# The last down projection in seven-product form with 128 by 256 accumulators, and the activation moved to where the up products leave PSUM

## The chip, the cores and the metric

The kernel runs on one core of a Trainium2 chip. The metric is device time in microseconds (us), the median of several executions; lower is better. The engines are TensorE (PE, with its weight loads as PEld), VectorE (DVE), ScalarE (ACT), GpSimd (POOL) and SyncE (SP, which issues most DMAs).

## The reference

Attention with a memory term gives 2304 tokens of 512 values; two feed-forward blocks follow. All arithmetic is float32.

```python
# x: [2304, 512] from attention
g = x @ moe_w_gate                                   # 512 -> 1536
x = (g * sigmoid(g) * (x @ moe_w_val)) @ moe_w_out   # 1536 -> 512
h = x @ moe2_w_in                                    # 512 -> 2048
h = where(h >= 1, h, where(h <= -1, 0, (h + 1)**2 / 4))
out = h @ moe2_w_out                                 # 2048 -> 512: the stage that is changed
```

## The kernel before, in words

Every float32 operand of a product is split into a high part (a cast to fp32r) and a low part (the rest), and each product is three fp32r matmuls (`PARTS`: low by high, high by low, high by high). The cast is made on ACT, the subtraction of the rest on DVE; `halves` and `split` do that.

After attention and a little early work the kernel has three long stages.

1. Gate and value products, from about 284 us: each block of 256 by 256 by (2 times 384 tokens) is made with seven products in place of eight (Strassen's scheme in Winograd's form): `chain` issues products 1 to 7 on PE, ACT copies partial sums from one PSUM bank to another, DVE adds. A chain takes three of the eight PSUM banks. `pair` prepares the weights (unpacks the numbers, makes four sums, splits).
2. Down products of the first block (`down`, line L1621), then `y_pieces`, which makes the seven sums of each token block.
3. The second block: up products by `chain` with kind "up" (L1540), 8 pairs `p` of weight columns by 3 token blocks `kb`; in its function `last` two of the four outputs are copied from PSUM by ACT (L1589), the others are already in SBUF, and `store` writes 48 tiles to DRAM (`h2s`). Then the last down projection, `down2`, for 6 groups of 384 tokens and 8 pairs `i` of hidden rows: load a tile back (L1659), Relu and Square on ACT (L1661, L1663), the clamping minimum on DVE (L1664), split (L1440 on ACT, L1443 on DVE), and 18 matmuls of 128 by 512 (L1675) into three banks. At the end of a group three copies (L1690) and stores. Its 16 weight blocks were unpacked, split and put in DRAM earlier (`parked`), and are read back whole (`whole`).

The order of all instructions is written out beforehand. A class `Plan` simulates the engines with fixed costs (for PE `e_pe(n, cols)`: n times (cols + 32)/2.4 ns, with 25 in place of 32 below 320 columns) and handover times (`LAT`), keeps the matmuls in the order of the program (`seq`), and gives every other instruction a due time worked back from the matmul that needs it, or from `by`. `gate(ahead)` holds a load back until PE is that many ns before its use. Each engine then runs its list in order, so a waiting instruction holds up those behind it. SBUF places are counted by tags: 25 places `X` of 6 KB for split operands, 7 flat tiles `T`, `raw`, `rw`, `wp`, `wA` for preparing weights, `su` for the chains' sums, and eight banks `mm`.

Of the kernel before, what the change touches and what calls it, by code (L numbers as in the profile page):

```python
# [19 lines left out]
P = 128  # L20
# [23 lines left out]
SET_AHEAD, PARK_AHEAD, H_AHEAD, H2_AHEAD, W_AHEAD, W2_AHEAD = 40000, 60000, 20000, 20000, 12000, 7000  # L44
# [107 lines left out]
class Plan:  # L152
# [4 lines left out]
    LAT = {"PE": 220, "ACT": 165, "DVE": 150, "POOL": 120, "SP": 650, "DMA": 950}  # L157
# [783 lines left out]
class Weights:  # L941
# [174 lines left out]
    def whole(self, plan, u, gate):  # L1116
        i = plan.inst("X")
        s = {"i": [i]}

        def load():  # L1120
            s["w"] = self.slab(i.slot, [P, 2, 512])
            self.nc.sync.dma_start(f32(s["w"]), u["home"])

        s["t"] = [plan.dma(None, [1456], load, [u["store"]], [i], behind=gate)]
        return s

    def pair(self, plan, srcs, behind, free, homes=None):
# [4 lines left out]
        places = [plan.inst("X"), plan.inst("X"), plan.inst("wh")]  # L1132
        s, w = {}, {}
        n = 2 * 512

        def load(j):
            if j == 0:
                s["raw"] = self.p["rw"].tile([P, 2 * n], U32, name="rw", tag=f"rw{i_raw.slot}")
            dst = s["raw"][:, j * n:(j + 1) * n].rearrange("p (k c) -> p k c", k=srcs[j].shape[1])
            nc.sync.dma_start(dst, srcs[j])  # L1140
# [47 lines left out]
        sub, add = nc.vector.tensor_sub, nc.vector.tensor_add  # L1188
# [4 lines left out]
                ("DVE", e_dve2(n), sign, [i_raw, i_W]), ("DVE", e_dve2(n), whole, [i_W]),  # L1193
                ("DVE", e_dve2(256), two(add, 4, 2, 3), [i_W]), ("DVE", e_dve2(256), two(sub, 2, 0, 2), [i_W]),
                ("DVE", e_dve2(256), two(sub, 5, 4, 0), [i_W]), ("DVE", e_dve2(256), two(sub, 6, 1, 5), [i_W]))
        for k, (on, took, fn, uses) in enumerate(steps):
            if homes and k < 6:
                continue
            t = [plan.add(on, took, None, fn, t, uses)]
            made[k] = t[0]  # L1200
        ends = [self.split(plan, None, [made[d]], lambda a=a, b=b: f32(W(a, b)), lambda j=j, m=(b - a) * 256: dst(j)[:, :, 0:m],
                           (b - a) * 256, [i_W, places[j]], behind=free)
                for j, (d, a, b) in enumerate(((7, 0, 3), (8, 3, 6), (9, 6, 7)))]
        at_ = ((0, 0), (0, 256), (2, 0), (1, 0), (1, 256), (1, 512), (0, 512))
        return {"t": [ends[j] for j, _ in at_], "i": [places[j] for j, _ in at_],
                "k": lambda k, part, j: w[at_[k][0]][:, part, at_[k][1] + j * P:at_[k][1] + (j + 1) * P]}

# [24 lines left out]
def tile_attention_two_moe(  # L1232
# [12 lines left out]
    nc.gpsimd.memset(half, 0.5)  # L1245
    xs = dram.tile([P, KT, NT], F32, name="xs")
    gv = [dram.tile([P, 2, GE * HB], F32, name=f"gv{j}") for j in range(2)]
    hs = [[dram.tile([P, 2, HB], F32, name=f"hs{i}_{g}") for g in range(NG)] for i in range(F1 // 2)]
    h2s = [[dram.tile([P, 2, HB], F32, name=f"h2s{i}_{g}") for g in range(NG)] for i in range(F2 // 2)]
# [118 lines left out]
    mm = ctx.enter_context(tc.tile_pool(name="mm2", bufs=1, space=PSUM, reuse_waits="tile"))  # L1368
    unused = [early[g][0]["slot"] for g in range(1, GE, 2)]
# [156 lines left out]

    def chain(S, x, kind, ends):
# [21 lines left out]
        def spot(name, place, j):  # L1549

            def get():
                if kind == "up":
                    return rt["get"]()[:, j]
                if name not in s:
                    s[name] = su.tile([P, HB], F32, name=name, tag=f"su{place.slot}")
# [17 lines left out]
        def last():  # L1573
# [4 lines left out]
            done = {0: [], 1: []}  # L1578
            for n, (T, j, src, i, t) in enumerate(parts):
# [232 lines left out]
```

## Time and profile before

| what | value |
|---|---|
| median of 3 runs | 1013.84 us (1013.26 to 1015.34) |
| the profiled execution's own time | 1013.86 us |
| its span in the profile | 1012.1 us |
| granted TensorE clock, mean | 0.996 of full speed |
| up products of the second block | 637.5 to 811.2 us |
| last down stage | 811.2 to 1008.2 us |

The profiled execution is 1.76 us longer than its span. Line numbers in the profile are those of the kernel before.

### The profile page before, as it was taken

Reading aid. Unit: us, or ns where it says so; the run is one execution under the profiler, and the core shown is the slowest. Engines: PE = TensorE matmul, PEld = TensorE weight load, DVE = VectorE, ACT = ScalarE, POOL = GpSimd, SP = SyncE. Lnnn points to the kernel's source line nnn. Section 1 sums busy time; section 2 is a strip of 40 time slices with the busy share of each in tenths; the row PEclk is TensorE's granted clock in tenths of the full one; section 3 lists DMA queues with packets and bytes.
Section 4 is the critical chain, followed back from the end, with each engine's and each line's share of the span. In section 5 each row is a group of like instructions: output and inputs, shape, how many; then the busy total and the mean of one; then the engine's idle time right before and its main releaser. Section 6 shows DMA issues by size and latency. Waiting matters only on the chain.

```text
span 1012.1 us, 16215 instructions
## 1 busy us (share of the span) xinstructions
PE 995.0 (98%) x5898; PEld 907.0 (90%) x5898; DVE 678.4 (67%) x1402; ACT 621.4 (61%) x1221; POOL 116.8 (12%) x165
## 2 busy tenths in 40 slices
PE   6999999999999999999999999999999999999998
PEld 6667787778999999999999999999999988888886
DVE  5899998872888878676467577776654346455541
ACT  3999888873566665655255445666554657566651
POOL 3543666630000000000000000000000000000000
PEclk9999999999999999999999999999999999999999
DMA  7867454214835463544975544356742696324430
GB/s 182 192 160 181 129 128 115 75 60 132 291 103 183 146 197 134 169 169 159 397 273 186 183 146 162 141 201 230 256 179 116 214 384 205 125 80 139 141 95 31
DMA packets 137248, 171.72 MB, mean 170 GB/s; under 512 B 67536, under 2 KB 99280, under 8 KB 137168
## 3 DMA queue, kind: packets, MB, share of 16 engines
q1 hardware_dynamic: 135838, 170.39, 51.5%
q8 instruction: 46, 0.75, 0.3%
q10 hardware_dynamic: 1330, 0.30, 0.2%
q14 instruction: 34, 0.28, 0.1%
HBM read 111.28 MB, written 59.38 MB: 169 GB/s over the span
## 4 chain that ended last, share of the span: by engine, by line
PE 92%; DMA 3%; ACT 2%; DVE 1%; SPq 1%; issue 0%; ACTq 0%; DVEq 0%
PE mm L1540 38%; PE mm L1675 19%; PE mm L1621 15%; PE av L911 4%; PE s L730 3%; PE mm L1317 3%; PE t L861 2%; PE av L903 2%; PE s L764 2%; DMA xr<-xs 1%; PE t L878 1%; ACT a L751 1%; DMA qn<-in_q_dram 1%; PE t L839 1%; PE tk L609 1%; PE tq L620 1%
## 5 line engine op out<-in xcount | busy, mean ns | idle before, releaser
L1540 PE MATMUL mm<-xw 128*128 128x384 f32 x1944 | 346.9, 334 | 1.4 <-ACT mm L1562 1.0
L1540 PEld LDWEIGHTS mm<-xw 128*128 128x128 f32 x1944 | 337.7, 188 | 2.2 <-ACT mm L1562 1.3
L1675 PE MATMUL mm<-xw 128*128 128x512 f32 x864 | 196.2, 389 | 0.0
L1675 PEld LDWEIGHTS mm<-xw 128*128 128x128 f32 x864 | 162.2, 188 | 33.6
L1621 PE MATMUL mm<-xw 128*128 128x384 f32 x864 | 150.1, 334 | 0.0
L1621 PEld LDWEIGHTS mm<-xw 128*128 128x128 f32 x864 | 149.8, 188 | 0.0
L751 ACT ACTIVATE a<-a,mn 128x256 f32<-128x256 f32 (+3 forms) x128 | 71.4, 565 | 4.0 <-DVE mn L744 3.7
L1664 DVE SCALAR_TENSOR_TENSOR t<-r,t 128x768 f32<-128x768 f32 x48 | 46.0, 958 | 38.0 <-ACT t L1663 38.0
L1443 DVE TENSOR_TENSOR xw<-t,xw 128x768 fp32r<-128x768 f32 x48 | 45.9, 957 | 37.2 <-ACT xw L1440 37.2
L1440 ACT CAST xw<-t 128x768 fp32r<-128x768 f32 x48 | 40.1, 834 | 40.6 <-DVE t L1664 40.6
L1540 PE MATMUL mm<-xw,wh 128*128 128x384 f32 x324 | 64.8, 334 | 0.0
L823 POOL TENSOR_SCALAR a<-a,r,one 128x128 f32<-128x128 f32 (+4 forms) x77 | 57.9, 763 | 44.0 <-DVE r L812 22.5
L1562 ACT COPY mm<-mm 128x384 f32<-128x384 f32 x54 | 25.1, 465 | 57.1 <-PE mm L1540 56.8
L744 DVE CUSTOM_DVE_ANT_0 a<-s,mask 128x128 f32<-128x128 f32 (+3 forms) x128 | 55.6, 483 | 6.3 <-PE s L730 6.2
L1540 PEld LDWEIGHTS mm<-xw,wh 128*128 128x128 f32 x324 | 56.9, 188 | 0.0
L515 ACT COPY R<-t 128x384 f32<-128x384 f32 (+2 forms) x97 | 44.9, 507 | 8.7 <-PE t L861 5.0
L1661 ACT ACTIVATE t<-r,half 128x768 f32<-128x768 f32 x48 | 44.9, 935 | 7.9 <-DMA r<-h2s 7.2
L911 PE MATMUL av<-R,vn 128*64 128x320 f32 (+3 forms) x384 | 47.8, 379 | 0.0
L911 PEld LDWEIGHTS av<-R,vn 128*64 128x64 f32 x384 | 28.1, 137 | 20.8 <-ACT R L515 0.4
L1440 ACT CAST xw<-h 128x768 fp32r<-128x768 f32 x36 | 29.7, 835 | 27.2 <-DMA h<-hs 14.7
L1443 DVE TENSOR_TENSOR xw<-h,xw 128x768 fp32r<-128x768 f32 x36 | 34.0, 954 | 14.9 <-ACT xw L1440 14.7
L1047 DVE TENSOR_TENSOR xw<-wp,xw 128x768 fp32r<-128x768 f32 x36 | 34.0, 954 | 12.1 <-ACT xw L1045 12.0
(160 smaller groups left out, 1471.2 us busy)
## 6 DMA issues: line engine op xcount, KB each, us to landing
h2s<-r SPq DMA_DIRECT2D x48, 384.0 KB
r<-h2s SPq DMA_DIRECT2D x48, 384.0 KB
raw<-in_moe_w_out_dram SPq DMA_DIRECT2D x28, 512.0 KB
park<-pk SPq DMA_DIRECT2D x28, 512.0 KB
hs<-h SPq DMA_DIRECT2D x33, 384.0 KB
h<-hs SPq DMA_DIRECT2D x33, 384.0 KB
xw<-park SPq DMA_DIRECT2D x24, 512.0 KB
xr<-xs SPq DMA_DIRECT2D x24, 384.0 KB
```

What stands on the lines that cost most here:

```text
L515: copy(dst(), src())
L744: nc.vector.tensor_tensor_reduce(a, st[f"s{h}{tag}"][:, at_[c]:at_[c] + kl[c]], self.mask0[:, 512 - kl[c]:512], -0.125, 3.0e38, ALU.add, A ...
L751: nc.scalar.activation(a, a, AF.Exp, bias=mn[:, o:o + 1], scale=-1.0, accum_out=sm[:, o:o + 1])
L823: eng.tensor_scalar(a, a, r, self.one, op0=ALU.mult, op1=ALU.mult)
L911: nc.tensor.matmul(o[rg][halves[h], c0:c1], V, r, start=False, stop=i == len(terms[rg]) - 1, tile_position=(0, h * 64), skip_group_check=True)
L1440: nc.scalar.copy(s["x"][:, :, 0], t())
L1443: nc.vector.tensor_sub(s["x"][:, :, 1], t(), f32(s["x"][:, :, 0]))
L1540: nc.tensor.matmul(o, S["k"](k, pw, j), x[k]["at"](px, j), start=begin and not (i or j), stop=j == 1 and i == 2, skip_group_check=True)
L1621: nc.tensor.matmul(o, u["k"](pw, m), h["at"](px, j), start=(p == 0 and j == 0 and n == 0), stop=(p == F1 // 2 - 1 and j == 1 and n == 2), ...
L1661: x1 = add_act(2 * HB, lambda raw=raw, t=t: nc.scalar.activation(t["get"](), raw["get"](), AF.Relu, bias=half, scale=0.5), [x], [raw["i"], ...
L1664: x1 = add_dve(2 * HB, lambda raw=raw, t=t: nc.vector.scalar_tensor_tensor(t["get"](), raw["get"](), 1.0, t["get"](), op0=ALU.max, op1=ALU ...
L1675: nc.tensor.matmul(o, h["at"](px, j)[:, m * P:(m + 1) * P], u["w"][:, pw], start=(i == 0 and j == 0 and n == 0), stop=(i == F2 // 2 - 1 an ...
```

## The change

The last down projection becomes seven products as well. A task is now a `batch`: 256 tokens (`n`, 9 chunks) by four row blocks of 128 of the weights (`b`, 4 of them). `split` is called for 768, 768 and 256 columns; `prod` goes over 2 row blocks, the 7 products and the 3 parts. A stationary operand is a 128 by 128 piece of tokens, the moving one is a 128 by 256 piece of weights, and the seven accumulators of 128 by 256 lie in half banks, four banks to a token chunk. DVE makes four token sums for a batch (three instructions), ACT and DVE split them; the weight sums are made in advance by `parked_pair` (8 pairs, 7 pieces each), written to DRAM and read back by `seven`. `clean` fills the halves that no matmul starts with zeros, `finish` combines the seven accumulators (one copy on ACT, four additions on DVE) and stores. The first two token chunks run interleaved, the other seven one after another.

The activation goes from the reading side to the end of `chain`: `bend` makes Relu and Square on ACT and the minimum on DVE, from PSUM for two of the four outputs and in SBUF for the other two (with DVE in place of ACT for the first step where `kb` is not 0). The `h2s` tiles that are stored now hold activated values.

Other parts of it: loads of `h` in `down` and of the batches are issued by ACT in place of SP; the weight parking of the last stage goes from the stage of the gates to spots set by due times there and in the down stage of the first block; the last two pairs `p` of the up stage alternate for each `kb`; `wA` and the chains' sums share one `su` tile.

```diff
-SET_AHEAD, PARK_AHEAD, H_AHEAD, H2_AHEAD, W_AHEAD, W2_AHEAD = 40000, 60000, 20000, 20000, 12000, 7000
+SET_AHEAD, PARK_AHEAD, H_AHEAD, H2_AHEAD, W_AHEAD, W2_AHEAD = 40000, 60000, 20000, 20000, 12000, 36000
-    LAT = {"PE": 220, "ACT": 165, "DVE": 150, "POOL": 120, "SP": 650, "DMA": 950}
+    LAT = {"PE": 220, "ACT": 165, "DVE": 150, "POOL": 120, "SP": 650, "DMA": 950, "QACT": 950}
...
+    def bend(n, t, src, deps, uses, by, dst=None, act=True):
+        dst = dst or t
+        if act:
+            x = add_act(n, lambda: nc.scalar.activation(t(), src(), AF.Relu, bias=half, scale=0.5), deps, uses, by=by)
+            x = add_act(n, lambda: nc.scalar.activation(t(), t(), AF.Square), [x], uses, by=by)
+        else:
+            x = plan.add("DVE", e_dve(n), None, lambda: nc.vector.tensor_scalar(
+                t(), src(), -1.0, 1.0, op0=ALU.max, op1=ALU.add), deps, uses, by=by)
+            x = add_act(n, lambda: nc.scalar.activation(t(), t(), AF.Square, scale=0.5), [x], uses, by=by)
+        return add_dve(n, lambda: nc.vector.scalar_tensor_tensor(
+            dst(), src(), 1.0, t(), op0=ALU.max, op1=ALU.min), [x], uses, by=by)
...
+            if kind == "up":
+                for j, (src, i, t) in enumerate(((lambda: P_("e"), i_e, t2), (lambda: P_("a"), i_a, t4))):
+                    done[0].append(bend(HB, lambda j=j: lf["get"]()[:, j], src, [t], [i, lf["i"]], by))
+                tmp = flat("b2")
+                done[1].append(bend(2 * HB, tmp["get"], rt["get"], [v1, v2], [rt["i"], tmp["i"]], by, rt["get"], not ends["kb"]))
...
-    def down2(g):
...
+    BANKS = ((0, 0), (1, 0), (3, 0), (3, 256), (2, 0), (1, 256), (2, 256))
+    SEVEN = (((0, 1, 0), (1, 3, 2), (3, 2, 6)), ((6, 4, 1), (4, 5, 4), (5, 6, 5)), ((2, 7, 3),))
...
+        d = add_dve(256, lambda: sub(R(4, 5), R(0, 1), R(1, 2)), x, i_r)
+        d = add_dve(512, both, [d], i_r)
+        d = add_dve(256, lambda: sub(R(7, 8), R(3, 4), R(6, 7)), [d], i_r)
+        t = [split(j, x if j == 0 else [d]) for j in range(3)]
+        def prod(j, prods):
+            for i, u in enumerate(us):  
+                for k, g, w in prods:
+                    bk, c = BANKS[k]
+                    o = acc(state, bk)[:, c:c + 256]
+                    for q, (pw, px) in enumerate(PARTS):
+                        nc.tensor.matmul(o, dst(j)[:, px, i, g - 1 - 3 * j], u["k"](w, pw),
+                                         start=b + i + q == 0 and k in OPEN,
+                                         stop=b == 3 and i == 1 and q == 2, skip_group_check=True)
...
+        state["clean"] = [add_act(256, lambda k=k: fill(k), [], [state["i"][k]], behind=gate(8000) if w_out else seq[-1:])
+                          for k in (1, 2, 3)]
...
+        t = add_act(256, lambda: nc.scalar.copy(one_(), state[0][:, 0:256]), [ends[0]], [i_b[0], one["i"]], by=by)
+        t = add_dve(512, lambda: add(O()[:, 0:4:3], one["get"]()[:, 0:1, 0:256].to_broadcast(two), B2(1)), [t, ends[1], ends[5]],
+                    [i_b[1], one["i"], i_o], by=by)
+        t = add_dve(512, lambda: add(O()[:, 1:3], O()[:, 3:4].to_broadcast(two), B2(2)), [t, ends[4], ends[6]], [i_b[2], i_o], by=by)
+        t = add_dve(256, lambda: add(O()[:, 3], O()[:, 2], state[2][:, 0:256]), [t], [i_b[2], i_o], by=by)
+        t = add_dve(512, lambda: add(O()[:, 1:3], O()[:, 1:3], B2(3)), [t, ends[2], ends[3]], [i_b[3], i_o], by=by)
...
-    for g in range(NG):
-        down2(g)
+    for some in ((0, 1), *((n,) for n in range(2, NT // (2 * P)))):
+        for n in some:
+            clean(states[n])
+        for b in range(4):
+            for n in some:
+                ends[n] = batch(n, b, states[n], n == NT // (2 * P) - 1)
+        for n in some:
+            finish(n, states[n], ends[n], n == NT // (2 * P) - 1)
```

## Rows read from the trace of the kernel before

**Rows 1.** The page, busy time of each engine and its share of the span

```profile
PE 995.0 (98%) x5898; PEld 907.0 (90%) x5898; DVE 678.4 (67%) x1402; ACT 621.4 (61%) x1221; POOL 116.8 (12%) x165
```

**Rows 2.** Chain of waits from 486 us on: start, length, what

```profile
637.50 173.71 PE mm L1540 x1002
811.22 4.12 PE mm L1675 x18
...
816.40 191.82 PE mm L1675 x846
...
1008.24 0.69 DVE oo L1690
```

**Rows 3.** Busy time by stage, with counts; clock, DMA share and GB/s last

```profile
283.70:486.70 203.00, 203.00 (x1171) 203.00 (x1172) 154.01 (x269) 119.37 (x220) 0.00 (x0) 1.00 0.48 166
...
637.50:811.20 173.70, 173.70 (x1004) 173.65 (x1003) 101.85 (x165) 102.36 (x186) 0.00 (x0) 1.00 0.55 192
811.20:1008.20 197.00, 197.00 (x871) 162.95 (x869) 93.35 (x102) 116.61 (x142) 0.00 (x0) 1.00 0.44 149
```

**Rows 4.** Groups by shape, PE: count, busy us, mean ns of one, idle before

```profile
L1675 PE MATMUL mm<-xw 128*128 128x512 f32 x864 | 196.2, 389 | 0.0
L1621 PE MATMUL mm<-xw 128*128 128x384 f32 x864 | 150.1, 334 | 0.0
```

**Rows 5.** The same for PEld: a load for an fp32r matmul, for a transpose

```profile
L1621 PEld LDWEIGHTS mm<-xw 128*128 128x128 f32 x864 | 149.8, 188 | 0.0
...
L861 PEld LDWEIGHTS t<-ident,a 128*128 128x128 f32 x224 | 26.1, 141 | 4.3 <-PE tp L682 1.0 <-ACT a L751 0.5 <-POOL a L823 0.5
```

**Rows 6.** Chain of waits, attention, 140 to 195 us: eight transposes

```profile
186.19 0.87 PE tk L609 x8
```

**Rows 7.** Groups by shape from 637.5 us on, DVE

```profile
L1664 DVE SCALAR_TENSOR_TENSOR t<-r,t 128x768 f32<-128x768 f32 x48 | 46.0, 958 | 38.0 <-ACT t L1663 38.0
L1443 DVE TENSOR_TENSOR xw<-t,xw 128x768 fp32r<-128x768 f32 x48 | 45.9, 957 | 37.2 <-ACT xw L1440 37.2
L1569 DVE TENSOR_TENSOR r<-r,mm 128x384 f32<-128x384 f32 x24 | 13.3, 554 | 33.9 <-PE mm L1540 29.5 <-ACT pk L1045 2.0 <-ACT wA L981 1.4
...
L1175 DVE TENSOR_TENSOR wp<-wp 128x256 f32<-128x256 f32 x27 | 11.1, 421 | 0.3
L1690 DVE COPY oo<-mm 128x512 f32<-128x512 f32 x12 | 8.3, 691 | 32.5 <-PE mm L1675 32.5
...
L1160 DVE TENSOR_SCALAR wp<-wp 128x1024 f32<-128x1024 f32 x6 | 4.2, 694 | 14.1 <-ACT wp L1157 14.1
```

**Rows 8.** Groups by shape from 637.5 us on, ACT

```profile
L1661 ACT ACTIVATE t<-r,half 128x768 f32<-128x768 f32 x48 | 44.9, 935 | 7.9 <-DMA r<-h2s 7.2 <-DMA xw<-park 0.6
L1663 ACT ACTIVATE t<-t 128x768 f32<-128x768 f32 x48 | 40.7, 847 | 1.3
L1440 ACT CAST xw<-t 128x768 fp32r<-128x768 f32 x48 | 40.1, 834 | 40.6 <-DVE t L1664 40.6
L1589 ACT COPY r<-mm 128x384 f32<-128x384 f32 x48 | 23.1, 481 | 18.2 <-PE mm L1540 17.6 <-DMA r<-h2s 0.6
...
L1169 ACT ACTIVATE wp<-rw 128x1024 int32<-128x1024 uint32 x6 | 6.9, 1152 | 0.0
...
L981 ACT ACTIVATE wA<-raw 128x512 f32<-128x512 f32 x6 | 4.1, 676 | 1.6 <-DMA raw<-in_moe_w_out_dram 1.5
...
L1045 ACT CAST wh<-wp 128x256 fp32r<-128x256 f32 x7 | 2.8, 407 | 1.2 <-PE mm L1540 1.2
```

**Rows 9.** Busy time of each engine in the densest 50 us of DVE

```profile
300.00:350.00 50.00, 50.00 (x291) 50.00 (x290) 42.33 (x77) 31.25 (x56) 0.00 (x0) 1.00 0.49 168
```

**Rows 10.** What PE waited for from 240 us on: total, times, longest

```profile
PE mm L1540 <- ACT mm L1562: 1.0, 1, 1.0
PE mm L1491 <- DVE xw L1443: 0.5, 1, 0.5
PE mm L1540 <- DVE xw L1443: 0.4, 1, 0.4
```

More of the change, by code (lines that the diff above doesn't have):

```diff
@@ L1114, in trio, with wide @@
         return out
[L1116 to L1127, printed above, removed]
+    def wide(self, plan, srcs, behind, combos, homes=None):
         nc = self.nc
         i_raw, i_W = None if homes else plan.inst("rw"), plan.inst("wp")
-        places = [plan.inst("X"), plan.inst("X"), plan.inst("wh")]
-        s, w = {}, {}
+        s = {}
         n = 2 * 512
@@ L1248, in tile_attention_two_moe @@
     hs = [[dram.tile([P, 2, HB], F32, name=f"hs{i}_{g}") for g in range(NG)] for i in range(F1 // 2)]
[L1249 removed]
+    h2s = [dram.tile([P, 2, NT], F32, name=f"h2s{i}") for i in range(F2 // 2)]
     wts = Weights(ctx, tc, dram)
@@ L1368, in tile_attention_two_moe, with shared, tile @@
     mm = ctx.enter_context(tc.tile_pool(name="mm2", bufs=1, space=PSUM, reuse_waits="tile"))
+    shared_ = {}
+    def shared():
+        if "t" not in shared_:
+            shared_["t"] = su.tile([P, SU * HB + 512], F32, name="su", tag="su")
+        return shared_["t"]
+    class Rest:
+        def tile(self, shape, dtype, **_):
+            return shared()[:, SU * HB:SU * HB + 512].bitcast(dtype)
+    wts.p["wA"] = Rest()
     unused = [early[g][0]["slot"] for g in range(1, GE, 2)]
@@ new lines, in clean, with fill, finish, O @@
+    def clean(state):
+        def fill(k):
+            c = 256 if k == 1 else 0
+            nc.scalar.copy(acc(state, k)[:, c:c + 256], zero.to_broadcast([P, 256]))
+        state["clean"] = [add_act(256, lambda k=k: fill(k), [], [state["i"][k]], behind=gate(8000) if w_out else seq[-1:])
+                          for k in (1, 2, 3)]
+    def finish(n, state, ends, last):
+        i_o, one = plan.inst("raw"), flat("p1")
+        s = {}
+        def O():
+            if "o" not in s:
+                s["o"] = wts.p["raw"].tile([P, 4, 256], F32, name="oo", tag=f"raw{i_o.slot}")
+            return s["o"]
+        B2 = lambda k: state[k].rearrange("p (j c) -> p j c", j=2)
+        one_ = lambda: one["get"]()[:, 0, 0:256]
+        add, by = nc.vector.tensor_add, clock[0] + 8000
+        i_b, two = state["i"], [P, 2, 256]
+        t = add_act(256, lambda: nc.scalar.copy(one_(), state[0][:, 0:256]), [ends[0]], [i_b[0], one["i"]], by=by)
[4 more added lines that the diff above has]
+        t = add_dve(512, lambda: add(O()[:, 1:3], O()[:, 1:3], B2(3)), [t, ends[2], ends[3]], [i_b[3], i_o], by=by)
+        def put(j):
+            o = n * 2 * P + (1 - j) * P
+            (nc.scalar if last and j else nc.sync).dma_start(
+                out[o:o + P, :], O()[:, 2 * j:2 * j + 2].rearrange("p j c -> p (j c)"))
+        for j in range(2):
+            if last and j:
+                t = plan.add("ACT", 450, None, lambda: put(1), [t], [i_o], by=by)
+                plan.add("QACT", 728, None, lambda: None, [t], [i_o], by=by)
+            else:
+                plan.dma(None, [728], lambda j=j: put(j), [t], [i_o], by=by)
@@ L1751, in tile_attention_two_moe, with park @@
             make(*todo[n + 2])
-    parks2 = [wts.parked(plan, out_rows(moe2_w_out, f), gate(PARK_AHEAD)) for f in range(F2)]
+    parks2 = []
+    def park(n, ahead, by):
+        for i in range(n):
+            parks2.append(wts.parked_pair(plan, [out_rows(moe2_w_out, 2 * len(parks2) + c) for c in range(2)], gate(ahead),
+                                          clock[0] + by + 2 * i * PARK_TURN))
+    park(2, 50000, -30000)
     yp = {}
@@ L1757, in tile_attention_two_moe @@
         yp[kb] = y_pieces(kb)
-    due = {p: clock[0] + p * long for p in range(F2 // 2)}
+    due = {p: clock[0] + (p * long if p < F2 // 2 - 1 else (p - 1) * long + long / NK) for p in range(F2 // 2)}
     def make2(p):
```

192 lines of the change are left out of this document (128 added, 64 removed).

## Prediction

> **What bounds the kernel now.** Read first the share of busy time [rows 1]: PE 98%, DVE 67%, ACT 61%. An average hides stages, so next comes the chain of waits [rows 2]: from 637.5 us to the end it is PE alone, one stretch of up products, then the down products (864 matmuls in 4.12 + 191.82 = 195.9 us, or 226.8 ns each), and only the last copy and store behind it. What PE waited for [rows 10] comes to 1.9 us in 770 us. So what a stage is worth is its matmuls, and anything that makes PE wait is added in full. Third, busy time by stage [rows 3]: PE is full in all of them at full clock (1.00, the 2.4 GHz level), while the last stage leaves DVE free for half of its time (93.35 of 197.0 us) and ACT for 40%. That room is what the change spends. In the up stage DVE and ACT have about 102 of 174 us each.
>
> **Matmuls.** Before: 6 groups x 8 pairs x 18 = 864 of 512 columns. After: 9 chunks x 4 batches x 2 row blocks x 7 products x 3 parts = 1512 of 256 columns. Columns fall by an eighth, from 442,368 to 387,072, but the number of matmuls and of weight loads rises by three quarters. So all hangs on the pace of a 128x256 matmul, and no fp32r matmul of that shape is in the trace. The nearest rows are 512 columns, 226.8 ns [rows 2, 4], and 384 columns, 150.1/864 = 173.7 ns [rows 4]. At 2.4 GHz the columns alone take 213.3 and 160 ns, so each matmul costs 13.5 ns more than its columns, whatever its length. For 256 columns that is 106.7 + 13.4 = 120.1 ns. The planner's own formula, which gives 226.7 and 173.3 for the two measured widths, has a smaller constant below 320 columns and says 117.1. I take the middle, 118.5: 1512 x 118.5 = 179.2 us, a gain of 16.7 (18.9 at 117.1; 14.3 at 120.1).
>
> **The weight load as the upper bound.** Each matmul brings a 128-column load. Its record is 188 ns [rows 5], yet at 384 columns the pairs follow every 173.7 ns, so records overlap and 188 is not the load's own pace. What that pace is, these matmuls don't show, since they are longer. The nearest row that does is a transpose, also 128 columns of weights: eight take 0.87 us, 109 ns each [rows 6], with a record of 141 ns [rows 5]. An fp32r load's record is 47 ns longer, so its pace lies between nothing that shows and 109 + 47 = 156 ns. At 156 the stage would take 236 us, a loss of 40; the gain would be gone, with the terms below, at (195.9 - 4.8)/1512 = 126.4 ns. I take the load as covered: 156 is a ceiling, and the one step in the trace that runs loads of 128 columns at their closest, the transpose, needs 109 ns with its own streaming in it, less than 118.5.
>
> Of the matmul's own part the traces and a rule differ. The rows above show 13.5 ns beside the columns at two widths. "TensorE: Matmul & The Clock Gate" of the Trainium skill, section "Back-to-back issue gap", gives N/2.4 + 2.5 ns for one isolated matmul after another when warm, and says that a stream with weight loads is set by both instructions. By its formula 512 columns would take 215.8 ns, which the 226.8 of the trace contradicts; by it the new stage would be 1512 x 109.2 = 165 us (an estimate from the page) and the sum 14 us lower than mine. The same page's section "LDWEIGHTS (loading the stationary operand)" gives P/1.2 ns, 107 ns for 128 columns; no run here shows it alone.
>
> **DVE and ACT in the last stage.** A batch on DVE: sums of 256, 512 and 256 columns, .421 + .691 + .421, and splits of 768, 768, 256, .957 + .957 + .421 [rows 7]: 3.87 us. `finish` adds 3 x .691 + .421 = 2.49 for a chunk. In all 36 x 3.87 + 9 x 2.49 = 161.7 us, 90% of 179.2 (before: 47%). Per batch PE needs 42 x 118.5 = 4.98 us, DVE 3.87 and a quarter of 2.49, 4.49. So DVE keeps ahead, with three batches in flight (turns of `rw`, `wp` and `su`), but narrowly. ACT's casts, .834 + .834 + .407 [rows 8] = 2.08 per batch, with fills and copies 4 x .407 a chunk, 89 us in all: free, even with 72 loads issued by ACT at the planner's 0.45 us. A load there waits for its tile to be free, and the next batch's casts stand behind it; they are due one batch later, so the cover is 5 us. I take 1.0 us of PE waits for the stage, between 0 and what the second rival gives.
>
> **Start, refill, tail.** At the start `clean` follows the beginning of the last up product, which lasts 6 x 173.7 ns = 1.04 us; three fills of .407 and the handover take 1.4 if ACT is free, 2.3 behind one long activation (.935). PE waits 0.4 to 1.3; I take 0.7. At the third token chunk the eight banks are all in use by the first two, so PE waits for `finish` of chunk 0: copy .407, additions 2.49, fill .407 and four handovers (0.15 to 0.22 in `LAT`), 4.0 us, under the 4.98 of chunk 1's last batch. But the due times of `finish` are counted from the end of both chunks, so one batch's 3.87 us of DVE work can come between: 7.9, a wait of 2.9. Between 0 and 2.9 I take 1.5. Later chunks have a whole chunk's time for this. At the end, before, one copy of .69 stood between the last matmul and the stores [rows 2]. After, copy, three additions and handovers (0.22 + .407 + .165 + .691 + .691 + .421 = 2.6) begin 12 matmuls (1.4 us) before the end, then comes the last addition: 1.2 + .69 = 1.9. That is 1.2 more, and less a little by the second queue for the last store: 1.1.
>
> **The up stage.** Removed: two copies of .481 a chain. Added on ACT: Relu and Square of 384 columns twice; at the copy's .481 for each pass of 384 columns, .088 more for the bias operand (.935 against .847 [rows 8]) and a little, some 1.1 for each output; then for 768 columns .935 + .847 where `kb` is 0, else .847. Net 3.0 for 8 chains, 2.1 for 16: 58 us. On DVE: 2 x .554 and .958, and for 16 chains at most .694 (a 1024-column row [rows 7]): up to 61 us. What leaves: six parkings ran here [rows 8], three activations of some .65 and five DVE steps of .42 to .69 each, about 12 us of ACT and 17 of DVE, and three sets of the old activation and split, 8 and 6. The first two batches come in with 4 and 8. ACT ends at 144 of 174 us (83%), DVE at 148 (85%). DVE was at 42.33 of 50 us [rows 9] without a wait of PE, so 85% is proven here; ACT never was above 63%, and its copies stand between products of one chain. PE issues two other products (2.08 us) before it needs the first copy; copy (.464 to .481) and two handovers take 0.85, and one activation ahead of it at most 1.15 [rows 8]. That just fits. Without that cover each chain loses some tenths; I take 0.5 in all.
>
> **Moved work.** 48 loads leave SP for 72 smaller ones on ACT, 33 of `down` go with them; 24 loads of `seven` (7 pieces of 256 columns, 2 parts, 128 partitions, 8 pairs: 14.7 MB) replace 16 (8.4 MB), begun 36 us before use in a stage at 0.55 of the DMA time [rows 3]. The weights' parking gets dearer (sums of weights) but moves to stages where PE never waited for it [rows 10]. I cost these at nothing; their cover is the 36 us, and a load that missed it would hold PE by the excess, some us once.
>
> **Sum,** against the profiled execution, 1013.86 us (the median of the runs is 1013.84, so no correction): -16.7 + 1.0 + 0.7 + 1.5 + 1.1 + 0.5 = -11.9, that is 1002.0. With 117.1 ns and no wait but tail and start: 996. With 120.1 and all waits at their upper ends (3.5 in the stage): 1009.
>
> **Rivals.**
> *The weight load sets the pace.* For it: the load's record is longer than the new matmul, and nothing in the trace runs a load every 120 ns. Against: the transposes at 109. Slower from 126.4 ns on; halfway to 156, at 138, it gives 1013.86 - 195.9 + 208.7 + 4.8 = 1031. Chance 7%.
> *DVE sets the pace of the last stage.* For it: 90% needed, and 42.33 of 50 [rows 9] is the most that it kept up; each batch passes ACT and DVE in turn. At 85% its 161.7 us take 190, and the time becomes 1013.86 - 195.9 + 190 + 3.3 = 1011. Against: in rows 9 it was not asked for more. Chance 13%.
> *ACT is late in the up stage.* Half a us for each of 24 chains gives back the whole gain: 1014. Chance 8%.
> *The fixed part shrinks at 256 columns* to 2.5 ns: 988. Two measured widths speak against it. Chance 3%.
> *Not a smaller stage at all:* sharing of `su` by chains and parking brings waits into the earlier stages, say 14 us, 1016. Nothing in the rows speaks for it. Chance 1%.
>
> **Chances.** My forecast has 68%, its own range is 996 to 1009. To hold 8 in 10 the range takes in the second rival: 995 to 1012. No change is within 0.2%, 2 us, about what a measurement of this kernel can tell. Faster: 68 + 13 + 3 and a little of the ACT rival, 85%. Same: 5%. Slower: 10%.
>
> **What would show it.** Right: matmuls of the new stage every 117 to 120 ns in the chain of waits, PE idle under 5 us from 640 us on, DVE at 85 to 92% and ACT under 60% there, the stage near 181 us, ACT at about 83% in the up stage. Wrong: a pace above 126 ns; idle time of PE before each batch that ends with DVE's split; idle of PE behind ACT's copies (L1562, L1566) in the up stage; a wait above 3 us at the third chunk or at the end.

## The result and the profile after

| | before | after |
|---|---|---|
| median of 4 runs each, on one chip | 1014.12 us (1013.26 to 1015.34) | 1028.72 us (1026.63 to 1030.33) |
| the profiled execution, and its span | 1013.86, 1012.1 us | 1030.33, 1028.5 us |
| moved to and from DRAM | 111.28 + 59.38 MB | 117.58 + 65.67 MB |

The ratio is 1.0142, with a 95% interval of 1.0119 to 1.0165: slower by 1.4%, above the predicted range (995 to 1012) where a gain was forecast. Lines have moved by the change: L1540 of before is L1612 of after, L1621 is L1697, and the new last stage is L1790.

First the page's shares of busy time, of after. PE fell from 98% [rows 1] to 96%, though it now has fewer columns to run.

```profile
PE 989.9 (96%) x6546; PEld 933.4 (91%) x6546; DVE 789.4 (77%) x1650; ACT 634.2 (62%) x1295; POOL 116.8 (11%) x166
```

Then the chain of waits of after from 450 us on (start, length, what). In before that chain was nothing but PE from 449.96 us to the last copy ([rows 2] shows it from 637.5 us on). Now there is a stretch of transfers from 465 to 522 us, and a second one at the seam of the up stage and the last stage.

```profile
449.96 12.49 PE mm L1612 x72
...
465.38 4.84 DMA park<-pk
470.32 4.15 DMA h<-hs
476.35 7.49 DMA h<-hs
485.83 7.79 DMA hs<-h
493.64 6.26 DMA h<-hs
499.99 5.75 DMA h<-hs
508.44 9.48 DMA park<-pk
517.93 3.94 DMA xw<-park
521.91 130.30 PE mm L1697 x741
652.22 135.25 PE mm L1612 x780
...
808.23 6.92 DMA rg<-h2s
...
833.25 8.62 DMA rg<-h2s
844.47 177.25 PE mm L1790 x1455
```

Busy time by stretch, of after: the length, then PE, PEld, DVE, ACT and POOL with their instruction counts, then granted clock, DMA share, GB/s. PE is full in the up stage up to 808 us, but for 0.55 us, and full after 850 us. It idles 6.3 us in 480 to 515, 3.6 in 515 to 530 and 10.3 in 795 to 850, and in these three of the five stretches the clock is below 1.00.

```profile
480.00:515.00 35.00, 28.67 (x150) 28.03 (x149) 17.25 (x27) 9.27 (x13) 0.00 (x0) 0.91 0.96 334
515.00:530.00 15.00, 11.38 (x55) 11.06 (x54) 8.23 (x11) 7.95 (x11) 0.00 (x0) 0.87 0.76 246
...
652.20:808.20 156.00, 155.45 (x897) 154.90 (x896) 123.86 (x202) 120.84 (x216) 0.00 (x0) 1.00 0.49 168
...
795.00:850.00 55.00, 44.66 (x259) 43.17 (x258) 31.60 (x57) 30.07 (x58) 0.00 (x0) 0.94 0.97 347
850.00:1000.00 150.00, 150.00 (x1252) 150.00 (x1252) 119.90 (x209) 69.03 (x119) 0.00 (x0) 1.00 0.48 149
```

The same view of before at those two places, which the prediction does not use. The DMA engines were already full from 480 to 515 us (share 1.01), with PE at work all the time.

```profile
480.00:515.00 35.00, 35.00 (x204) 35.00 (x203) 16.43 (x27) 12.54 (x20) 0.00 (x0) 1.00 1.01 384
...
795.00:850.00 55.00, 55.00 (x267) 48.45 (x266) 27.97 (x34) 37.94 (x53) 0.00 (x0) 1.00 0.85 307
```

PE's timeline of after (start, length, what, idle before it). A batch is 36 + 6 matmuls, and batches start every 5.04 us from 851.99 to the last at 1018.31, across every chunk's seam: 42 matmuls in 5.04 us are 120.0 ns each. The one batch that runs slower is the one behind the wait.

```profile
485.13 3.71 PE L1612 MATMUL mm<-xw 128*128 128x384 f32 x12 [2.92 <-ACT mm L1634]
...
834.20 1.31 PE L1612 MATMUL mm<-xw 128*128 128x384 f32 x6 [0.99 <-DVE r L1643]
835.35 4.47 PE L1790 MATMUL mm<-xw 128*128 128x256 f32 x36
...
844.47 6.96 PE L1790 MATMUL mm<-xw 128*128 128x256 f32 x36 [3.94 <-DVE r L1596]
...
851.99 4.48 PE L1790 MATMUL mm<-xw 128*128 128x256 f32 x36
...
857.03 4.48 PE L1790 MATMUL mm<-xw 128*128 128x256 f32 x36
...
1022.63 0.88 PE L1790 MATMUL mm<-xw,x 128*128 128x256 f32 x6
```

From this the difference is made up in four terms, two of which are losses that get a name for what follows. The stage's matmuls: 1512 x 120.0 ns = 181.4 us in place of 195.9, -14.5. **Loss A:** the up stage begins at 652.22, not 637.50, +14.7. **Loss B:** from there the up stage needs 174.8 us (637.50 to 811.22, and the 1.06 behind 815.34 that belong to it) and the new stage 181.4, which would end PE at 652.22 + 174.8 + 181.4 = 1008.4 us; it ends at 1022.63 + 0.88 = 1023.5, +15.1. The tail behind PE is 5.0 us, not 3.9, +1.1. Sum +16.4; the spans differ by 16.4. Loss A and B of each experiment below are worked out in the same way, from the start of its up stage and the end of its last matmul.

### The profile page after: what moved, and what is told of

Its sections match the earlier page's. It is cut to its first block, busy times and chain, and to the rows that moved or that the text cites. A ratio compares the mean times of both kernels' runs of the same rounds, so it can differ in the third digit from the quotient of the medians.

```text
span 1028.5 us, 17913 instructions
## 1 busy us (share of the span) xinstructions
PE 989.9 (96%) x6546; PEld 933.4 (91%) x6546; DVE 789.4 (77%) x1650; ACT 634.2 (62%) x1295; POOL 116.8 (11%) x166
## 3 DMA queue, kind: packets, MB, share of 16 engines
HBM read 117.58 MB, written 65.67 MB: 178 GB/s over the span
## 4 chain that ended last, share of the span: by engine, by line
PE 83%; DMA 9%; DVE 3%; ACT 2%; SPq 1%; issue 1%; ACTq 0%; DVEq 0%
PE mm L1612 33%; PE mm L1790 17%; PE mm L1697 13%; PE av L912 4%; PE s L731 3%; PE mm L1363 3%; DMA h<-hs 2%; PE t L862 2%; DMA xr<-xs 2%; PE av L904 2%; PE s L765 2%; DMA rg<-h2s 2%; DMA park<-pk 1%; PE t L879 1%; DMA qn<-in_q_dram 1%
## 5 line engine op out<-in xcount | busy, mean ns | idle before, releaser
L1612 PE MATMUL mm<-xw 128*128 128x384 f32 x1944 | 349.4, 335 | 10.1 <-DVE r L1643 6.0
L1612 PEld LDWEIGHTS mm<-xw 128*128 128x128 f32 x1944 | 338.9, 188 | 12.3 <-DVE r L1643 7.0
L1790 PE MATMUL mm<-xw 128*128 128x256 f32 x1296 | 163.9, 286 | 3.9 <-DVE r L1596 3.9
L1790 PEld LDWEIGHTS mm<-xw 128*128 128x128 f32 x1296 | 160.5, 195 | 4.1 <-DVE r L1596 4.1
L1697 PE MATMUL mm<-xw 128*128 128x384 f32 x864 | 153.5, 339 | 7.0 <-DMA xw<-park 7.0
L1697 PEld LDWEIGHTS mm<-xw 128*128 128x128 f32 x864 | 152.6, 191 | 7.7 <-DMA xw<-park 7.7
L1767 ACT CAST xw<-rg 128x768 fp32r<-128x768 f32 x72 | 59.9, 834 | 77.3 <-PE mm L1790 48.6
L1768 DVE TENSOR_TENSOR xw<-rg,xw 128x768 fp32r<-128x768 f32 x72 | 68.6, 955 | 19.9 <-ACT xw L1767 19.9
L1612 PE MATMUL mm<-xw,wh 128*128 128x384 f32 x324 | 65.0, 334 | 0.4 <-ACT r L1635 0.4
L1498 ACT CAST xw<-h 128x768 fp32r<-128x768 f32 x36 | 30.0, 836 | 53.6 <-DMA h<-hs 51.3
L1501 DVE TENSOR_TENSOR xw<-h,xw 128x768 fp32r<-128x768 f32 x36 | 34.3, 955 | 32.2 <-ACT xw L1498 32.1
L1612 PEld LDWEIGHTS mm<-xw,wh 128*128 128x128 f32 x324 | 56.9, 188 | 0.7 <-ACT r L1635 0.7
L1634 ACT COPY mm<-mm 128x384 f32<-128x384 f32 x54 | 25.1, 465 | 41.2 <-PE mm L1612 40.5
L912 PEld LDWEIGHTS av<-R,vn 128*64 128x64 f32 x384 | 28.1, 137 | 20.8 <-ACT R L516 0.4
L1166 DVE TENSOR_TENSOR wp<-wp 128x256 f32<-128x256 f32 x104 | 43.2, 420 | 1.2 <-DMA raw<-in_moe_w_out_dram 0.5
L731 PE MATMUL s<-K,S 64*128 64x256 f32 (+3 forms) x256 | 40.0, 446 | 0.1
L1046 ACT CAST xw<-wp 128x768 fp32r<-128x768 f32 x36 | 29.5, 832 | 11.5 <-DVE wp L1166 6.2
```

The source lines that it names most:

```text
L731: nc.tensor.matmul(out[h][:, at_[c]:at_[c] + kl[c]], st["S"][halves[h], c * P:(c + 1) * P], st["K"][halves[h], 0:kl[c]], start=True, stop= ...
L912: nc.tensor.matmul(o[rg][halves[h], c0:c1], V, r, start=False, stop=i == len(terms[rg]) - 1, tile_position=(0, h * 64), skip_group_check=True)
L1166: return lambda: fn(f32(W(o, o + 1)), f32(W(x, x + 1)), f32(W(y, y + 1)))
L1612: nc.tensor.matmul(o, S["k"](k, pw, j), x[k]["at"](px, j), start=begin and not (i or j), stop=j == 1 and i == 2, skip_group_check=True)
L1697: nc.tensor.matmul(o, u["k"](pw, m), h["at"](px, j), start=(p == 0 and j == 0 and n == 0), stop=(p == F1 // 2 - 1 and j == 1 and n == 2), ...
L1767: t = add_act(256 * (b - a), lambda: nc.scalar.copy(dst(j)[:, 0], R(a, b)), deps, [*i_r, i_x[j]])
```

## Experiments

Theory 1 (order): loads that ACT issues are counted by the planner on a queue of their own (`QACT`), as if they had the full rate beside SP's transfers; they have not, so they land late, and ACT and DVE, which run their lists in order, wait for them in front of work that PE needs. Theory 2 (amount): the split weight sums (14.7 MB stored and read where it was 8.4) do not fit where the DMA engines are already full. Theory 3 (compute): the activation at the end of `chain` makes ACT and DVE late. Counting is done in the planner's simulation, so an edit of a count changes the order of the instructions and not the transfers. "Before" is the kernel before on the same chip: the median of 4 runs beside after, of 7 beside e9 to e12, one run beside the others. Of the experiments, e10 and e12 have 4 runs, the others one. The times of e1, e4 and e11 fell into a range that was expected for a theory, that of e10 0.07 us outside one, and that of e12 into the range for "another cause"; those of e2, e6 and e7 fell between two ranges, and those of e3, e5, e8 and e9 outside all.

| run | us | before | loss A | loss B |
|---|---|---|---|---|
| after | 1028.72 | 1014.12 | 14.7 | 15.1 |
| e1_h_on_sp | 1017.84 | 1013.31 | 4.7 | 12.6 |
| e2_one_dma | 1020.77 | 1013.31 | 11.4 | 8.8 |
| e3_loads_on_sp | 1021.78 | 1013.31 | 8.6 | 12.7 |
| e4_activation_only | 1013.32 | 1013.31 | -0.9 | |
| e5_batch_early | 1022.89 | 1014.56 | 7.4 | 15.0 |
| e6_batch_counted | 1014.18 | 1014.56 | 8.3 | 5.4 |
| e7_half_weights | 1011.41 | 1014.56 | 7.2 | 3.7 |
| e8_park_later | 1044.14 | 1014.56 | 7 + 20.8 | 15.7 |
| e9_half_both | 1016.01 | 1013.64 | 9.8 | 5.7 |
| e10_split_on_read | 1007.07 | 1013.64 | 4.0 | 2.2 |
| e11_h_on_act_only | 1020.09 | 1013.64 | 6.3 | |
| e12_park_gate | 1008.05 | 1013.26 | -0.8 | 8.4 |

Loss A of e1, e3, e5, e6 and e7, which have the same edit in the down stage but are planned anew for what follows it, lies between 4.7 and 8.6. So a step of less than some 4 us in one loss, in a single run, is not read as an effect.

**e4: the activation alone**, the kernel before with `bend` at the end of the up chains and the last stage's own activation removed.

```diff
+            if kind == "up":
+                for j, (src, i, t) in enumerate(((lambda: P_("e"), i_e, t2), (lambda: P_("a"), i_a, t4))):
+                    done[0].append(bend(HB, lambda j=j: lf["get"]()[:, j], src, [t], [i, lf["i"]], by))
+                tmp = flat("b2")
+                done[1].append(bend(2 * HB, tmp["get"], rt["get"], [v1, v2], [rt["i"], tmp["i"]], by, rt["get"], not ends["kb"]))
...
-            x1 = add_act(2 * HB, lambda t=t: nc.scalar.activation(t["get"](), t["get"](), AF.Square), [x1], [t["i"]])
...
-            h = halves(t["get"], t["i"], [x1])
+            h = halves(raw["get"], raw["i"], [x])
```

> The kernel before, with only the activation moved to the end of the up chains; the last stage keeps its 864 matmuls of 512 columns without the activation. Compute theory: ACT at 80 to 90 percent in the up stage makes PE wait there, 4 us or more, 1018 or more. Queue and traffic theories: the up stage loses under 2 us, 1012 to 1016.

Measured: 1013.32 beside 1013.31. Busy time in its up stage:

```profile
636.60:810.30 173.70, 173.70 (x1004) 173.65 (x1003) 146.60 (x247) 142.64 (x258) 0.00 (x0) 1.00 0.54 189
```

PE has no gap, with DVE at 84% and ACT at 82% of the stretch. Theory 3 falls for the up stage, and so does the rival "ACT is late in the up stage".

**e1: only the loads of `h` in `down` back on SP.**

```diff
-                x = plan.add("ACT", 450, None, lambda t=t, i=i: nc.scalar.dma_start(t["get"](), hs[i][g]), [t_hs[i, g]],
+                x = plan.dma(None, [2.85 * HB], lambda t=t, i=i: nc.sync.dma_start(t["get"](), hs[i][g]), [t_hs[i, g]],
                              [t["i"]], behind=gate(H_AHEAD))
-                x = plan.add("QACT", 2.85 * HB, None, lambda: None, [x], [t["i"]])
```

> Only the loads of h in the first block's down stage go back from ACT to SP. Queue theory (loads issued by ACT run beside SP's transfers although the plan counts each queue at full rate, so they land late and hold ACT's list): PE's loss between 462 and 522 us, 14.7 us, falls to 3 or less; the 17 us at the start of the last stage stay, so 1014 to 1018. Traffic theory (too many bytes at these spots, whichever queue carries them): the 14.7 us stay, 1026 to 1031. Compute theory (ACT and DVE are overloaded there): no change, 1026 to 1031.

Measured: 1017.84; loss A fell from 14.7 to 4.7. What an ACT-issued load does is seen in the timeline of ACT, of after:

```profile
476.35 0.33 ACTq L1685 DMA_DIRECT2D h<-hs  x1
...
483.86 0.83 ACT L1498 CAST xw<-h 128x768 fp32r<-128x768 f32 x1 [4.42 <-DMA h<-hs]
483.87 0.33 ACTq L1685 DMA_DIRECT2D h<-hs  x1
484.60 0.47 ACT L1634 COPY mm<-mm 128x384 f32<-128x384 f32 x1
```

The load took 7.5 us; the plan gives it 1.1 and 0.95 for landing. The cast stands 4.42 us. Behind it wait the next load's issue and the copy L1634, and for that copy PE waits 2.92 us (485.13 in PE's timeline). From 283 to 637 us ACT waits 51.3 us for these loads in after, 18.4 in e1 and 14.7 in before.

What is left of loss A in e1 are two waits of PE. One (3.12 us) ends with the split of an operand, which stands behind L1574, and that waited for a load (`v<-gv`); the other (2.17 us) ends with a load of weights (`xw<-park`). The DMA share from 480 to 515 us is 1.04 there.

**e11: the same part alone**, put into the kernel before.

```diff
-                x = plan.dma(None, [2.85 * HB], lambda t=t, i=i: nc.sync.dma_start(t["get"](), hs[i][g]), [t_hs[i, g]],
+                x = plan.add("ACT", 450, None, lambda t=t, i=i: nc.scalar.dma_start(t["get"](), hs[i][g]), [t_hs[i, g]],
                              [t["i"]], behind=gate(H_AHEAD))
+                x = plan.add("QACT", 2.85 * HB, None, lambda: None, [x], [t["i"]])
```

> The kernel before, with only the 33 h loads of the first block's down stage issued by ACT, counted beside SP's as in the changed kernel. If the queue alone costs, whatever else runs there: that stage loses 5 us or more, 1018 or more. If it costs only together with the new weight traffic: within 3 us of the kernel before, 1012 to 1016.

Measured: 1020.09, +6.4, with no other part of the change. Its waits of PE and its chain:

```profile
PE mm L1540 <- ACT mm L1562: 3.9, 2, 2.9
...
478.43 7.37 DMA h<-hs
...
643.78 173.68 PE mm L1540 x1002
```

The load takes 7.37 us and PE waits for ACT's copy, as in after; ACT's waits for these loads come to 49.1 us from 283 to 637 us, where before had 14.7. This is the part of theory 1 that is shown from both sides. The part costs 6.3 us alone, and taking it out of after gives back 6.1 to 10.0 (by the 4.7 to 8.6 that the runs with e1's edit still lose), so the two sides agree within the spread.

**e2: ACT issues, but the planner counts on one queue**, `"QACT"` changed to `"DMA"` in three places.

```diff
-            x.append(plan.add("QACT", 728, None, lambda: None, [t], i_r))
+            x.append(plan.add("DMA", 728, None, lambda: None, [t], i_r))
```

> ACT issues the same loads, but the plan counts all transfers in one place, so the order of instructions allows for shared transfers. Queue theory, with the plan's order as the cause: both losses shrink, 1000 to 1015. If it is the issuing from ACT itself that hurts, in whatever order: 1022 to 1031. Traffic theory: 1022 to 1031.

Measured: 1020.77, between the two expectations. Loss B fell to 8.8, loss A only to 11.4, a step within the spread. Yet ACT's waits for the `h` loads fell from 51.3 to 24.2 us, though ACT still issues them: for these waits the count matters. PE's longest wait is now another one, 7.8 us (L1697 for the split L1501), and it leads back to a load that SP issues (`v<-gv`). So whether issuer or count sets loss A is not separated.

**e3: batch loads on SP too**, on top of e1. This changes two things for the batches: SP issues their loads, and the planner counts them with SP's, as in e6 below.

```diff
-            nc.scalar.dma_start(s["r"][:, i, 0:4].rearrange("p (f t) x -> p f (t x)", f=2),
+            nc.sync.dma_start(s["r"][:, i, 0:4].rearrange("p (f t) x -> p f (t x)", f=2),
                                 h2s[2 * b + i][:, :, n * 2 * P:(n + 1) * 2 * P])
...
-            x.append(plan.add("QACT", 728, None, lambda: None, [t], i_r))
```

> The h loads and the 72 loads of the batches all go by SP. Queue theory: both losses shrink; if the start of the last stage also loses nothing, 999 to 1006. Traffic theory for the start of the last stage (14.7 MB of weights there): its 17 us stay, 1014 to 1018. Compute theory: no change in either, 1026 to 1031.

Measured: 1021.78, outside all three ranges. Loss B is 12.7, as in e1 (12.6), but with other waits. PE's waits for the additions that end the up chains, 6.4 and 3.4 us in e1, fell to 0.6. In their place PE waits 7.6 us once, for a split of a batch: its load is issued by SP behind three loads of weights (829.26), and the first sum waits 9.67 us for it. So the right count alone does not cure B; with the loads in SP's list they stand behind the weights there.

**e5: batch loads allowed earlier**, e1 with one constant.

```diff
-SET_AHEAD, PARK_AHEAD, H_AHEAD, H2_AHEAD, W_AHEAD, W2_AHEAD = 40000, 60000, 20000, 20000, 12000, 36000
+SET_AHEAD, PARK_AHEAD, H_AHEAD, H2_AHEAD, W_AHEAD, W2_AHEAD = 40000, 60000, 20000, 45000, 12000, 36000
```

> The h loads on SP as in the first run, and the batches' loads allowed 45 us before their use in place of 20. If the start of the last stage loses its 14 us because the first batches' loads come in the middle of the weights' burst, the loss halves or better: 1004 to 1011. If it is the amount of data in that stretch, loading some of it earlier gives little: 1014 to 1019.

Measured: 1022.89, loss B 15.0. More lead does not help: the first batch load is issued at 776.7 us, where e1 issues it at 797.2, and B is no smaller.

**e6: batch loads counted with SP's**, e1 with `"QACT"` changed to `"DMA"` for them alone.

> The h loads on SP, and the plan counts the transfers of the batches' loads, still issued by ACT, with SP's. If the plan's order is the cause (sums that wait for a late load stand ahead of the chain's additions on DVE), PE's waits for the chain's additions go and the time falls by 5 us or more from the first run's 1017.8: 1006 to 1013. If the amount of data is the cause, no more than 3 us: 1015 to 1019.

Measured: 1014.18; loss B from 12.6 to 5.4, at a DMA share of 1.03 in 795 to 850 (0.96 in e1). With ACT issuing, the order that comes from the false count is more than half of B. Beside e3, where the count is right too and B is 12.7, it is the issuer that differs: for the batches SP was the worse one here.

**e7: half of the weights' data read back.** e1, in which the low parts of the last stage's weights are not read and the high parts stand in for them.

```diff
-                None, [2.85 * (b - a) * 256],
-                lambda j=j, a=a, b=b: self.nc.sync.dma_start(f32(tile(j)), u["home"][:, :, a * 256:b * 256]),
+                None, [2.85 * (b - a) * 128],
+                lambda j=j, a=a, b=b: self.nc.sync.dma_start(f32(tile(j)[:, 0]), u["home"][:, 0, a * 256:b * 256]),
```

> The h loads on SP, and only the high parts of the last stage's weights are read back (7.3 MB in place of 14.7) and stand in for the low parts; the matmuls are as many. Amount of data as the cause: the loss at the start of the last stage falls from 14 to under 5 us, 1004 to 1008. Order alone as the cause, with the queue at any load: 1012 to 1018.

Measured: 1011.41; loss B from 12.6 to 3.7. The DMA share in 795 to 845 is 0.81, where e1 had 0.96 and after 1.01:

```profile
795.00:845.00 50.00, 48.19 (x331) 47.23 (x331) 38.17 (x67) 29.99 (x56) 0.00 (x0) 1.00 0.81 271
```

So the larger part of B goes by less data with the false count as it was, or by a right count with the data as they were, if ACT issues the loads. This fits a loss that needs both full DMA engines and an order that lets a late transfer hold up PE's work; the order was planned anew in each run, so the two are not wholly apart. In after PE's waits at that place are these; the additions L1643 and L1596 end the up chains, and stand in DVE's list behind the batch sums, which wait for `rg`:

```profile
PE mm L1612 <- DVE r L1643: 6.0, 3, 2.6
PE mm L1790 <- DVE r L1596: 3.9, 1, 3.9
```

DVE's timeline of after shows it: the sum waits 6.11 us for the load, and L1596 comes three instructions later.

```profile
841.99 0.42 DVE L1779 TENSOR_TENSOR rg<-rg 128x256 f32<-128x256 f32 x1 [6.11 <-DMA rg<-h2s]
842.33 0.55 DVE L1593 TENSOR_SCALAR b<-r 128x768 f32<-128x768 f32 x1
842.80 0.68 DVE L1763 TENSOR_TENSOR rg<-rg 128x512 f32<-128x512 f32 x1
843.40 1.01 DVE L1596 SCALAR_TENSOR_TENSOR r<-mm,r 128x384 f32<-128x384 f32 x2
```

**e9: and half stored**, e7 in which the low parts are not written to DRAM either.

```diff
-            ends.append(plan.dma(None, [2.85 * n], lambda a=a, b=b, dst=dst: self.nc.sync.dma_start(
-                home[:, :, a * 256:b * 256], f32(dst())), [t], [i_w], by=by))
+            ends.append(plan.dma(None, [2.85 * n / 2], lambda a=a, b=b, dst=dst: self.nc.sync.dma_start(
+                home[:, 0, a * 256:b * 256], f32(dst()[:, 0])), [t], [i_w], by=by))
```

> The half-weights run, and the low parts of the last stage's weights are not written to DRAM either (7.3 MB less written while they are prepared); the matmuls are as many. If the 7 us that the first block's down stage lost in that run come from the amount of data there, they fall to under 3, and the time is 1002 to 1007. If not, 1009 to 1013.

Measured: 1016.01, outside both ranges; loss A 9.8, no smaller than e7's 7.2. The stored amount alone does not set loss A: theory 2 fails at that place in this form. The stores remain as many (32), and the DMA engines are as full (share 1.01 in 480 to 515).

**e8: the parking one token block later**, e1 with `kb == 0` changed to `kb == 1` at the two `park(3, ...)`.

> The h loads on SP, and the last six weight pairs of the last stage are prepared one token block later in the first block's down stage, away from the reading of that stage's own 12 weight blocks. If the 4.7 us that this stage still loses come from these transfers meeting, they go: 1012 to 1014. If not, or if the work then meets the up stage's weights: 1017 to 1022.

Measured: 1044.14. Loss A comes to 27.9 us: 7 of it as in e1 and the runs made from it, and 20.8 from a new wait that stands at the start of the up stage: the up weights are prepared late. In the order of the program the parking now stands in front of them, and it uses the same `rw` and `wp`; this reading was not tried further.

```profile
PE mm L1612 <- ACT xw L1046: 20.5, 1, 20.5
```

**e10: sums stored unsplit.** e6, in which the seven weight pieces of a pair go to DRAM as plain float32, in one 0.9 MB store, and ACT and DVE split them after reading; 7.3 MB each way in place of 14.7, and the parking loses its four splits a pair.

```diff
+        home = self.dram.tile([P, 7 * 256], F32, name=f"park2_{len(plan.tasks)}")
+        ends = [plan.dma(None, [1.42 * 7 * 256], lambda: self.nc.sync.dma_start(home, W(0, 7)), [made[3]], [i_W], by=by)]
...
+            t = plan.dma(None, [1.42 * (b - a) * 256],
+                lambda j=j, a=a, b=b: self.nc.sync.dma_start(f32(tile(j)[:, 1]), u["home"][:, a * 256:b * 256]),
+                u["store"], [places[j]], behind=gate)
+            ts.append(self.split(plan, None, [t], lambda j=j: f32(tile(j)[:, 1]), lambda j=j: tile(j),
+                                 (b - a) * 256, [places[j]]))
```

> The whole computation, with the h loads on SP, the batches' transfers counted with SP's, and the last stage's weight sums sent through DRAM unsplit (7.3 MB each way in place of 14.7); ACT and DVE split them after reading, 2.1 and 2.3 us for each of 8 pairs. Data theory: losses of some 4 us at the start of the last stage and 3 in the down stage, 1001 to 1007, faster than the kernel before by 0.7 to 1.3 percent. Compute theory (the 19 us more on DVE around the start of the last stage hold PE): 1009 or more.

Measured: 1007.07 (1004.50 to 1007.87, 4 runs) beside 1013.64 (7 runs): ratio 0.9932, 0.9913 to 0.9951, faster than before, by 0.7%. Losses 4.0 and 2.2; the 1009 or more of the compute theory did not come. The change beside e6, a single run of 1014.18, is the unsplit store and the split after reading. Its chain (the up stage is L1601, the last stage L1778):

```profile
506.82 134.70 PE mm L1685 x768
641.51 156.05 PE mm L1601 x900
...
818.11 39.60 PE mm L1778 x330
```

**e12: the parking's loads held back, its due times set back and set closer**, on top of e10.

```diff
-PARK_TURN = 7500
+PARK_TURN = 5000
...
-            park(3, 25000, 0)
+            park(3, 0, 15000)
...
-            park(3, 25000, -10000)
+            park(3, 0, 20000)
```

> The split-on-read version, with the last six weight pairs' loads held back until PE is past 512 and 537 us (they were let in 25 us ahead of that), and their due times moved back by 15 to 35 us. Data theory for the down stage: the stretch of 480 to 515 us is full of transfers already in the kernel before (384 GB/s), so that any byte added there is paid for in PE time; without the added loads PE's loss in that stage falls from 4 to under 1.5 us, 1002 to 1005. If the loss has another cause: 1006 to 1009. If the later parking meets the up stage's first weights: 1010 or more.

Measured: 1008.05 (1006.25 to 1009.03, 4 runs) beside 1013.26: 0.9944, 0.9927 to 0.9961. Loss A is gone: the up stage begins at 636.72. Loss B grew from 2.2 to 8.4, so nothing was won. Its windows at both places:

```profile
480.00:515.00 35.00, 34.83 (x201) 34.51 (x200) 18.22 (x26) 14.73 (x20) 0.00 (x0) 1.00 1.02 381
795.00:845.00 50.00, 45.42 (x316) 44.45 (x316) 41.87 (x72) 34.48 (x64) 0.00 (x0) 0.97 0.67 220
```

In the first the DMA engines are as full as ever (1.02) and PE hardly idles, as in before (1.01): full engines need not cost PE anything; what they carry and who waits for it decides. In the second they are not full (0.67), and DVE is at 84%. There PE waits 3.05 us for an addition that ends an up chain, and the 36 matmuls from 817.80 us take 5.97 us in place of 4.48. Why the last stage of e12 begins at 817.96, as that of e10 (818.11) does, with an up stage that began 4.8 us earlier, was not tried further.

## Why the prediction was wrong

- **The step that failed is "Moved work ... I cost these at nothing."** In its place the runs showed +29.8 us (A and B), most of it traced to transfers that landed late, against a gain of 14.5. Three of its grounds were false. The first, "begun 36 us before use in a stage at 0.55 of the DMA time" is a mean over 174 us; at the stage's seam it was 0.85 already in before, over 795 to 850 us. The second, "stages where PE never waited for it", is no measure of room: 480 to 515 us was full already, at 384 GB/s, and PE simply had not been the one to pay. The third: a late load does not "hold PE by the excess, some us once": the instruction that waits for it stands first in ACT's or DVE's list, with work for PE behind it, several times over.
- **Loss A** came for about half from loads issued by ACT and counted apart (6.1 to 10.0 of 14.7 go when they return to SP; e11: +6.4 from them alone). The rest hangs on when and in which form the weights are parked (e12 removes it). In e1 both waits that are left end with a transfer, which speaks for the transfers; but e9's smaller stores did not help, and no run takes away the parking's work on ACT and DVE alone, so this stays open.
- **Loss B** came from weights and batch loads meeting at the seam, in an order made from a false count (e6 and e7 each remove more than half; e5 excludes the lead). A right count is not enough by itself: in e3, where SP issues the loads behind the weights, B stays at 12.7.
- **Matmuls.** The mechanism was right, the pace mis-sized: 120.0 ns, not 118.5, so -14.5 and not -16.7. What a matmul costs beside its columns holds at a third width (13.3 ns here); the planner's smaller constant, with which I took the middle, does not. The 188 ns record of a weight load (195 in the new stage) set nothing: the rival "weight load sets the pace" falls, and so does the 2.5 ns one. The formula that the prediction set beside these rows, the one in "TensorE: Matmul & The Clock Gate" of the Trainium skill, section "Back-to-back issue gap", which is given there for isolated matmuls, does not give the pace of this stream: 109.2 ns, against 120.0 measured.
- **DVE in the last stage:** 119.90 of 150 us, 80%, where 90% was worked out; PE never waits for it after 850 us. That rival falls. The work was sized rightly: the groups of that stretch add up to 133.7 us, 89%. But records of neighbouring instructions overlap (L1763 ends at 843.48, L1596 begins at 843.40), so a sum of records is more than the engine's busy time. ACT 46%, under the 60% that were said.
- **Other waits 1.0, start 0.7, refill 1.5:** nothing of them is seen; the first matmul of the stage follows the last up product at once (835.35), and no seam of chunks breaks the 5.04 us. (The 3.94 us before the second batch are part of loss B.) **Up stage 0.5:** nothing in e4, 0.55 in after. **Tail 1.1:** 1.1.
- So the terms that were costed would have given 1013.9 - 14.5 + 1.1 = 1000.5 us, near the 1002.0. That these came out 1.5 below the sum is partly luck: the smaller gain and the waits that did not come nearly cancel. The error of the result is in the part that was not costed. A slower kernel had been given 10%, most of it for causes that did not act: the weight load as the pace gave 1031, close to the 1028.72, but the pace was 120.0 ns and not 138. Sharing of `su` (1016, 1%) was not taken out by any run; no wait of PE in after ends with an instruction that writes `su`.

## What to carry to other kernels

Cost a moved or enlarged transfer in the stretch where it will run, at the width of a few transfers, not by a stage's mean: read the DMA share there, and where it is 1, ask what stands behind whoever waits for the late one. A second issuing engine added no bandwidth here, and a planner that gives it a rate of its own puts waits at the head of in-order engines. Where store and reload are the bottleneck and ACT or DVE have room, store the smaller form and expand it after reading. Here three repairs together turned +1.4% into -0.7%: the `h` loads back on SP (e1), the right count for the batch loads (e6, level with before: 1014.18 beside 1014.56), and the unsplit store (e10).

## What the runs showed of the hardware

**One rate for all issuers.** In 480 to 515 us the runs in which both SP and ACT issue loads there (after, e2, e11) moved 334 to 373 GB/s, those with SP alone 376 to 400. A 384 KB load of ACT's took 7.5 us there, one of 256 KB 8.6 us at the seam. The Trainium skill, "Trainium Kernel Development and Optimization", section "Key Constraints", says that transfers issued from several engines run interleaved on the same 16 DMA engines and that a further issuer saves issue time only. The rates agree: none with two issuers was above those with one. What the issue time was worth no run shows.

**A wait can cost more than its length.** Right after PE's longer waits in after (2.92 to 3.94 us) the granted clock is lower, and matmuls run slower. By stretch, then from PE's timeline:

```profile
485.00:490.00 5.00, 4.87 (x20) 4.88 (x21) 2.95 (x4) 2.69 (x5) 0.00 (x0) 0.69 0.89 291
...
840.00:845.00 5.00, 1.06 (x7) 0.86 (x6) 3.01 (x6) 2.08 (x5) 0.00 (x0) 0.81 1.05 392
845.00:850.00 5.00, 5.00 (x26) 5.00 (x25) 4.54 (x9) 2.48 (x5) 0.00 (x0) 0.51 0.64 186
```

```profile
490.78 4.32 PE L1697 MATMUL mm<-xw 128*128 128x384 f32 x24
...
512.55 5.73 PE L1697 MATMUL mm<-xw 128*128 128x384 f32 x24 [3.41 <-DMA xw<-park]
...
817.05 3.42 PE L1612 MATMUL mm<-xw 128*128 128x384 f32 x18 [2.62 <-DVE r L1643]
...
821.34 3.29 PE L1612 MATMUL mm<-xw 128*128 128x384 f32 x18
```

0.51 is about the 1.2 GHz level. The 36 matmuls that begin at 844.47 take 6.96 us, not 4.48: a wait of 3.94 cost 6.4. The 24 at 512.55 take 5.73, not 4.32, and the 12 at 485.13 take 3.71, where 12 take 2.24 in before. Not every wait does this: behind the 2.62 us at 817.05, at a granted clock of 1.00, 18 matmuls take 3.42 us, where 18 without a wait take 3.29. In 480 to 530 us PE idled 9.95 us, and loss A is 14.7; the slower matmuls behind its three waits explain about 4.5 of the difference (1.5, 1.4, and 1.6 for the 741 from 521.91, which take 130.30 us, 128.71 in e1).
